# A piece of the first K load goes ahead of wq in a cached GQA decode kernel

## The chip, the cores and the metric

One core of one Trainium2 chip (trn2), in a decode kernel with grouped-query attention (GQA): 16 query heads share 8 heads of K and V. The metric is the device time of one launch in microseconds (us), median over runs. All runs quoted here are of the fast state; a ratio is the mean time of one kernel's fast runs over that of the other's of the same rounds, so it is not quite the ratio of the medians that stand beside it.

## The reference, cut to what matters

```python
# A: x (1,1,448), wq (448, 4096), 16 query heads, 8 KV heads, cache 65536 long, head width 256, all bf16
q = x @ wq
scores = einsum(q, k_cache) * 256 ** -0.5     # k_cache, v_cache: (1, 8, 65536, 256), 268 MB each
a = einsum(softmax(scores), v_cache) @ wo     # wo (4096, 448)
b = token_mlp(layernorm(x))                   # small
out = g * a + (1 - g) * b                     # g = sigmoid(sum(x * gate_w))
```

One token reads two caches of 268 MB. Everything else is small.

## The kernel before

The cache is handled in 32 blocks of 16,384 positions (128 tokens for each of 128 partitions). SP, the engine that issues nearly all DMAs, alternates K and V loads of 8.39 MB. PE, the matmul engine, transposes K in 8 chunks of 16 tokens, forms the scores, and at the end of the block multiplies with V. A K load waits until the first four chunks of the block before are transposed, a V load until the products with the V block before are done. The first block is special: its K comes in two halves, and its V buffer holds wq until the q-projection is over.

```python
@block.sync
def _(eng):
    eng.dma_start(wq_a..., A_wq[0:384]...).then_inc(sem_wq, 16)      # 3072 KB
    eng.dma_start(wq_b,    A_wq[384:448]...).then_inc(sem_wq, 16)    # 512 KB
    for j in range(NP):                                              # 32 blocks
        last = j == NP - 1
        if j >= 1:
            eng.wait_ge(sem_tr[NB - 1], BODY * (j - 1) + DC)         # BODY 8, DC 4
        if j == 0:
            load(kring, A_k_cache, j, HV, NV, 0, sem_k)              # first half of K, 64 tokens
            load(kring, A_k_cache, j, 0, HV, 0, sem_kb)              # second half
        ...                                                          # (cut: last block)
        else:
            load(kring, A_k_cache, j, 0, NV, HV * (j % 2), sem_k)
        if j == 0:
            eng.wait_ge(s_q, 1); eng.wait_ge(s_hb, 1)                # q done: wq's place is free
        else:
            eng.wait_ge(sem_pv, j)
        load(vbuf, A_v_cache, j, ...)
        ...                                                          # (cut: wo, output)

@block.tensor
def _(pe):
    ...                                      # (cut) columns of x
    pe.wait_ge(sem_wq, 32)
    ...                                      # q-projection: 128 matmuls, then s_q
    ...                                      # h row, s_h; clears
    with nc.Fori(...):                       # blocks
        def transposes(k, c, j, u16, x2):    # chunk k of a block
            if k == 0:
                pe.wait_ge(sem_k, u16)       # 16 at block 0
            if k == DC:
                pe.wait_ge(sem_kb, 16)
            ...
```

The softmax here doesn't subtract the row's maximum and nothing guards it: scores larger than these inputs give would overflow.

## Time and profile before

| | before |
|---|---|
| median of 3 runs | 1266.03 us (1266.0 to 1266.64) |
| span of the profiled run | 1264.0 us |
| bytes moved, mean rate | 544.39 MB, 431 GB/s |
| PE, PEld (PE's weight loads), ACT (scalar engine), DVE (vector engine) busy | 73%, 69%, 43%, 33% |
| mean granted clock of PE | 0.842 |

Read it from the bottom: no compute engine is busy all the time, while the DMA row shows nine tenths in every slice but the last. The prediction shows the lines.

### The profile page before, as it was taken

The numbers are of one execution on the slowest core, as the hardware profiler recorded it, in microseconds if no ns is written. First come the engines' busy times: TensorE is split into PE (matmuls) and PEld (weight loads), VectorE is DVE, ScalarE is ACT, GpSimd is POOL, SyncE is SP. The second block draws the span as 40 slices with busy tenths as digits, with TensorE's granted clock in tenths as the row PEclk, the third lists the DMA queues.
The fourth block names the chain that finished last, engine by engine and source line by source line (L and its number), as shares of the span: only waits on it lengthen the run. The fifth ranks groups of instructions, "written<-read, shape, count | busy, mean of one in ns | idle before, by whom it ended". The sixth has DMA issues, their size and how long they took to land.

```text
span 1264.0 us, 38850 instructions
## 1 busy us (share of the span) xinstructions
PE 917.0 (73%) x17114; PEld 868.4 (69%) x17114; DVE 422.5 (33%) x764; ACT 538.2 (43%) x788; POOL 0.9 (0%) x7
## 2 busy tenths in 40 slices
PE   3876678766778667786676876758767688676688
PEld 2766668766677666786666876658766578666687
DVE  2433344333444333443222332323322233332233
ACT  1443345533355433454333553335533355433455
POOL 0000000000000000000000000000000000000000
PEclk9887788787898887987888987889887888877999
DMA  9999999999999999999999999999999999999998
GB/s 411 428 434 436 433 431 431 431 438 431 433 433 433 433 431 438 425 433 440 431 436 429 431 431 433 440 433 433 431 431 431 438 436 433 431 433 431 431 427 367
DMA packets 11623, 544.39 MB, mean 431 GB/s; under 512 B 1369, under 2 KB 1628, under 8 KB 2908
## 3 DMA queue, kind: packets, MB, share of 16 engines
q1 hardware_dynamic: 11522, 544.22, 99.7%
q8 instruction: 8, 0.13, 0.0%
q10 hardware_dynamic: 90, 0.01, 0.0%
q14 instruction: 3, 0.02, 0.0%
HBM read 544.22 MB, written 0.00 MB: 431 GB/s over the span
## 4 chain that ended last, share of the span: by engine, by line
DMA 70%; PE 29%; issue 1%; SPq 0%; DVEq 0%; DVE 0%; ACT 0%; ACTq 0%
DMA kring<-in_A_k_cache_dram 68%; PE kst L298 24%; PE sps L318 4%; DMA wo_sb<-in_A_wo_dram 2%; PE acc L358 0%; SPq L231 0%; SPq L265 0%; SPq L228 0%; SPq L226 0%; PE prj L405 0%; PE acc L347 0%; DVEq L92 0%; DVE out_row L634 0%; ACT pT L658 0%; ACTq L658 0%
## 5 line engine op out<-in xcount | busy, mean ns | idle before, releaser
L298 PE MATMUL kst<-ident,kring 128*128 128x128 f32 x4096 | 563.7, 299 | 304.9 <-DMA kring<-in_A_k_cache_dram 294.1
L669 ACT ACTIVATE ktT<-kst 128x1024 bf16<-128x1024 bf16 x512 | 500.0, 1021 | 667.3 <-PE kst L298 666.5
L298 PEld LDWEIGHTS kst<-ident,kring 128*128 128x128 f32 x4096 | 514.0, 156 | 314.8 <-issue 312.2
L569 DVE COPY ktT<-kst 128x1024 bf16<-128x1024 bf16 x512 | 354.2, 692 | 765.0 <-PE kst L298 742.0
L318 PEld LDWEIGHTS sps<-qcur,ktT 128*128 128x128 bf16 x8192 | 237.8, 96 | 4.1 <-issue 1.6
L318 PE MATMUL sps<-qcur,ktT 128*128 128x2 bf16 x8192 | 236.6, 163 | 1.3 <-issue 1.3
L358 PE MATMUL acc<-vbuf,pT 128*2 128x256 bf16 x4080 | 140.4, 305 | 3.8 <-issue 3.3
L358 PEld LDWEIGHTS acc<-vbuf,pT 128*2 128x2 bf16 x4080 | 105.2, 93 | 30.6 <-issue 3.8
L658 ACT ACTIVATE pT<-sps 128x32 f32 x256 | 51.8, 202 | 16.4 <-PE sps L318 16.4
L347 PE MATMUL acc<-pT,ones_sq 128*128 128x32 bf16 x256 | 11.7, 178 | 12.3 <-ACT pT L658 12.3
L347 PEld LDWEIGHTS acc<-pT,ones_sq 128*128 128x128 bf16 x256 | 8.6, 96 | 15.2 <-ACT pT L658 14.9
L675 ACT ACTIVATE z_b<-z_b 128x448 bf16<-128x448 bf16 x14 | 8.1, 577 | 20.5 <-DVE z_b L556 20.4
L575 DVE COPY accs<-acc 128x288 f32<-128x288 f32 x8 | 3.7, 458 | 38.5 <-PE acc L358 38.5
L394 PEld LDWEIGHTS acc<-sel,accs 128*64 128x64 f32 x112 | 10.8, 214 | 0.9
L394 PE MATMUL acc<-sel,accs 128*64 128x1 f32 x112 | 11.4, 260 | 0.0
L431 PE MATMUL acc<-vbuf 42*128 42x42 bf16 x1 | 0.2, 214 | 8.3 <-DMA b_b<-in_B_b_dram 8.3
L405 PE MATMUL prj<-wo_sb,oTn 128*1 128x112 bf16 x128 | 3.7, 244 | 3.1 <-DVE oTn L600 2.9
L431 PEld LDWEIGHTS acc<-vbuf 42*128 42x128 bf16 x1 | 0.1, 102 | 8.4 <-DMA b_b<-in_B_b_dram 8.4
L562 DVE TENSOR_TENSOR gu<-wtmp,z_b 128x448 bf16<-128x448 bf16 x14 | 5.5, 393 | 1.0
L554 DVE TENSOR_TENSOR z_b<-u_b,wtmp 128x448 bf16<-128x448 bf16 x14 | 5.5, 393 | 1.0
L550 DVE TENSOR_TENSOR z_b<-wtmp,u_b 128x448 bf16<-128x448 bf16 x14 | 5.5, 393 | 1.0
L548 DVE TENSOR_TENSOR wtmp<-u_b 128x448 bf16<-128x448 bf16 x14 | 5.5, 392 | 1.1
(89 smaller groups left out, 82.5 us busy)
## 6 DMA issues: line engine op xcount, KB each, us to landing
kring<-in_A_k_cache_dram SPq DMA_DIRECT2D x4, 4096.0 KB, 24.3
vbuf<-in_A_v_cache_dram SPq DMA_DIRECT2D x1, 6144.0 KB, 25.7
wo_sb<-in_A_wo_dram SPq DMA_DIRECT2D x7, 448.0 KB, 27.6
vbuf<-in_A_wq_dram SPq DMA_DIRECT2D x1, 3072.0 KB, 10.2
vbuf<-in_A_v_cache_dram SPq DMA_DIRECT2D x1, 1024.0 KB, 27.8
vbuf<-in_A_v_cache_dram SPq DMA_DIRECT2D x1, 768.0 KB, 28.9
vbuf<-in_A_wq_dram SPq DMA_DIRECT2D x1, 512.0 KB, 10.9
vbuf<-in_A_v_cache_dram SPq DMA_DIRECT2D x31, 29.7
```

Source lines behind the costliest of these rows:

```text
L298: ins = pe.transpose(kst[:, b, i * P:(i + 1) * P], kring_f[:, at + NT * (k % DC) + 4 * b + i, :], ident[:, :])
L318: ins = pe.matmul(sps[:, par, 2 * nt:2 * nt + 2], ktT[:, par, b, ntl * DH + dj:(ntl + 1) * DH:2], qcur[:, dj, :], start=(dj == 0), stop=(d ...
L347: pe.matmul(acc[:, DENC:SELC], ones_sq[:, :], pT[:, r, :], start=False, stop=(r == BODY - 1), skip_group_check=True)
L358: ins = pe.matmul(acc[o:o + REP, 0:DH], pT[:, r, 2 * nt:2 * nt + 2], vbuf[:, n, :], start=False, stop=False, skip_group_check=True)
L394: ins = pe.matmul(dst[hh * HP:(hh + 1) * HP, i:i + 1], accs[:, i:DH:2 * REP], sel[:, hh:hh + 1], start=False, stop=True, skip_group_check= ...
L548: vec.tensor_tensor(W, U, U, op=ALU.mult)
L550: vec.tensor_tensor(Z, W, U, op=ALU.mult)
L554: vec.tensor_tensor(Z, U, W, op=ALU.add)
L569: vec.tensor_copy(ktT[:, k % KTB, b, :], kst_b[:, b, :]).then_inc(sem_ev[b], 1)
L658: act.activation(pT[:, bass.ds(p0 + k % DC, 1), :].rearrange("p o n -> p (o n)"), sps[:, k % 2, 0:2 * NT], AF.Exp, scale=scale).then_inc(s ...
L669: act.activation(ktT[:, k % KTB, b, :], kst_b[:, b, :], AF.Copy).then_inc(sem_ev[b], 1)
L675: act.activation(z_b[:, :], z_b[:, :], AF.Tanh).then_inc(s_tanh, 1)
```

## The change

The intent: let the first bytes of K arrive first, so that the long work on K is not behind the 3.67 MB of wq. The first half of K is cut in two loads; the first of them, 32 of 64 tokens per partition (2.10 MB), is issued ahead of wq, the rest behind it. PE gets a wait for the new semaphore ahead of its loop.

```diff
+    NLEAD = 32
+        sem_lead = new_sem("sem_lead")
         def _(eng):
-            eng.dma_start(wq_a..., A_wq[0:WF * P, :]...).then_inc(sem_wq, 16)
-            eng.dma_start(wq_b, A_wq[WF * P:DM, :]...).then_inc(sem_wq, 16)
 ...
                 if j == 0:
-                    load(kring, A_k_cache, j, HV, NV, 0, sem_k)
+                    load(kring, A_k_cache, j, HV, HV + NLEAD, 0, sem_lead)
+                    eng.dma_start(wq_a..., A_wq[0:WF * P, :]...).then_inc(sem_wq, 16)
+                    eng.dma_start(wq_b, A_wq[WF * P:DM, :]...).then_inc(sem_wq, 16)
+                    load(kring, A_k_cache, j, HV + NLEAD, NV, 0, sem_k)
                     load(kring, A_k_cache, j, 0, HV, 0, sem_kb)
 ...
+            pe.wait_ge(sem_lead, 16)
             x2_reg = pe.alloc_register("x2_reg")
```

More of the change, by code (lines that the diff above doesn't have):

```diff
@@ L225, in _ @@
         def _(eng):
-            eng.dma_start(wq_a.rearrange("p j n -> p (j n)"),
-                          A_wq[0:WF * P, :].rearrange("(p j) n -> p (j n)", p=P)).then_inc(sem_wq, 16)
-            eng.dma_start(wq_b, A_wq[WF * P:DM, :].rearrange("r (a n) -> (r a) n", a=2)
-                          ).then_inc(sem_wq, 16)
             def load(dst, cache, j, n0, n1, at, sem):
@@ L238, in _ @@
                 if j == 0:
-                    load(kring, A_k_cache, j, HV, NV, 0, sem_k)
+                    load(kring, A_k_cache, j, HV, HV + NLEAD, 0, sem_lead)
+                    eng.dma_start(wq_a.rearrange("p j n -> p (j n)"),
+                                  A_wq[0:WF * P, :].rearrange("(p j) n -> p (j n)", p=P)).then_inc(sem_wq, 16)
+                    eng.dma_start(wq_b, A_wq[WF * P:DM, :].rearrange("r (a n) -> (r a) n", a=2)
+                                  ).then_inc(sem_wq, 16)
+                    load(kring, A_k_cache, j, HV + NLEAD, NV, 0, sem_k)
                     load(kring, A_k_cache, j, 0, HV, 0, sem_kb)
```

## The prediction

> **What bounds the kernel now.** I read the page from the top: engines, slices, queues. The reader is to see that no compute engine is near full and that the DMA row is.
>
> ```profile
> PE 917.0 (73%) x17114; PEld 868.4 (69%) x17114; DVE 422.5 (33%) x764; ACT 538.2 (43%) x788; POOL 0.9 (0%) x7
> ...
> DMA  9999999999999999999999999999999999999998
> ...
> DMA packets 11623, 544.39 MB, mean 431 GB/s; under 512 B 1369, under 2 KB 1628, under 8 KB 2908
> ...
> q1 hardware_dynamic: 11522, 544.22, 99.7%
> ```
>
> K and V cache alone are 2 x 8 x 65536 x 256 x 2 bytes = 537 MB of these 544 MB. 544.39 MB at 431 GB/s is 1263 us, the whole span (1264.0). So the time is bytes over rate, plus the little that the ends cost. The chain of waits agrees if it is read with care: it gives 68% to K loads and 24% to the transposes of L298, but these alternate only because a K load is issued when the transposes have freed its buffer.
>
> ```profile
> 1.67 21.40 DMA kring<-in_A_k_cache_dram
> 23.06 4.34 issue
> 27.41 6.17 PE kst L298 x32
> ...
> 38.79 34.06 DMA kring<-in_A_k_cache_dram
> 72.85 0.13 issue
> 72.97 5.59 PE kst L298 x32
> ...
> 83.77 27.79 DMA kring<-in_A_k_cache_dram
> ```
>
> A full K load is 8.39 MB, 19.5 us at 431 GB/s. The one issued at 83.77 takes 27.79 us, so it stood in the queue for about 8 us before its bytes moved. That is the reserve: PE could release a buffer 8 us later (less the start-up of a transfer) and no DMA engine would pause. I therefore do not read the 24% as PE time to be won.
>
> Where is DMA not full? The table of stretches (us, PE, PEld, DVE, ACT and POOL busy, clock, DMA share, GB/s) answers:
>
> ```profile
> 0.00:4.00 4.00, 0.43 (x5) 0.29 (x5) 2.08 (x11) 0.69 (x1) 0.91 (x7) 1.00 0.65 197
> 4.00:12.00 8.00, 0.21 (x1) 0.10 (x1) 2.56 (x8) 0.60 (x1) 0.00 (x0) 1.00 1.01 427
> 12.00:24.00 12.00, 4.69 (x132) 3.87 (x132) 2.65 (x15) 1.69 (x3) 0.00 (x0) 1.00 1.01 436
> 24.00:53.50 29.50, 24.36 (x404) 23.74 (x408) 13.88 (x26) 17.13 (x25) 0.00 (x0) 0.99 1.03 439
> 53.50:73.00 19.50, 6.95 (x129) 3.95 (x121) 0.53 (x2) 0.00 (x0) 0.00 (x0) 0.59 0.99 426
> ```
>
> Only the first 4 us fall short (197 against some 433, so about 2.2 us lost), and the last 6 us after the final V bytes. In 4 to 73 us, the whole stretch that the change can touch, DMA is at 426 to 439 although PE idles. A change of order there can't win time; it can only lose it by opening a gap.
>
> **What the Trainium skill says.** "DMA: Bandwidth & Descriptors", section "Where 436 GB/s comes from", gives 435 GB/s as the fabric ceiling; the trace agrees, 431 over the span, so there is no headroom of rate. The same page, "Queues, rings and completion order", says each DMA engine takes descriptors in ring order and that the completion count lands when the slowest engine has. The trace agrees: wq (3072 KB, issued 0.74) lands after 10.2 us, the first K half (4096 KB, issued 1.67) after 21.4, the second K half after 30.6: in the order of issue. So moving an issue moves landings and not the sum. "Runtime: NRT & Kernel Launch", section "Terms", says that an engine's instruction memory is refilled in 16 KiB blocks; the trace has 8 packets of 0.13 MB on the instruction queue, 16 KB each. I use this below for the 4.34 us of "issue".
>
> **The change part by part.**
>
> 1. The issue order. Before: wq (3.15 MB), rest of wq (0.52), K first half (4.19), K second half (4.19). After: K lead (32 of its 64 tokens per partition, 128 x 32 x 512 bytes = 2.10 MB), wq, rest of wq, K rest (2.10), K second half. The sum to the end of K's first half is 7.86 MB in both, so the K rest lands where the K half landed, at 23.1 us, and everything behind it is unmoved too.
>
> 2. What it adds: one DMA issue on SP, 0.41 us by those at 0.74 and 1.20, beside a queue that is filled for tens of us; 128 more row packets (two of 16 KB where one of 32 KB was) and 16 completion writes, 144 on 11623. If the 1369 packets under 512 B cost anything visible the rate could not be 431 throughout; I put under 0.1 us.
>
> 3. What the lead buys: nothing that I can find. PE's new wait for it stands after the q-projection and ahead of the loop, and the loop's first block still waits for the count of the old K semaphore (16 at block 0), which now the K rest raises. The transposes can't begin on the lead alone. The new wait is met long before: by the GB/s of the stretches (0.79 MB by 4 us, then 0.427 MB per us) the lead's 2.10 MB are in at 4 + 1.31/0.427 = 7.1 us, and PE gets there past 20.
>
> 4. What it costs: wq comes 2.10 MB later, 2.10/0.43 = 4.9 us. Its last part landed at 1.20 + 10.9 = 12.1, so now at about 17.0. The q-projection began at 12.58, held by the copy of xcol and not by wq; now wq holds it, so the delay is 17.0 - 12.6 = 4.4 us. The 128 matmuls of L441 and L443 end at 16.16 before, 20.6 after; the V load, issued at 17.54 behind the q and h steps, goes out at about 22.0.
>
> Is that delay on the path? First test: V must be in the queue before the K second half ends, at 32.8. Reserve before 15 us, after 11. Second: PE enters the loop at 22.3 instead of 17.9. Before, it could have begun at 23.06 but did so at 27.41; I take the 4.34 us for the first fetch of the loop's instructions (the queue shows instruction packets in 18 to 19, 24 to 25 and 30 to 31 us). If that fetch starts when PE arrives, the transposes start 4.4 us later, at 31.8, and the next K load goes out at 43.2 instead of 38.79. V and the wo load keep the queue filled until 53.5 (wo issued 17.91, 35.6 to landing). Reserve 10 us, before 15. Third: the next V load goes out when PE is done with block 0, at 63.58; 4.4 later is 68.0, and K block 1 lands at 72.85. Reserve 4.9 us, before 9.3. After that PE has to wait for K at 72.85 as before (it idled 6.85 us there, now some 2.5), and from 72.97 on the two kernels are the same. The delay is eaten by idle time of PE.
>
> Sum: 0 from bytes, +0.1 for packets, 0 from the delay: 1266.0 + 0.1 = 1266.1 us.
>
> **Rivals.**
> A. The lead starts PE early and the first block ends sooner. For it: transposes are the longest item of PE (563.7 us), and PE idles 9.5 us ahead of the first. Against: the old wait is kept, and even a PE 5 us earlier would only issue K block 1 sooner into a queue with 15 us of work. Worth 0; time 1266.
> B. The delay starves the queue. The third reserve is the thin one, 4.9 us less the 2 us or so that a transfer needs to its first bytes (the first packets of the kernel end near 2 us, issued at 0.74). If PE's later start grows by more instruction stalls (there are others of 3.33 and 2.38 us in block 0), a gap of 1 to 4 us opens once: 1267 to 1270, 0.1% to 0.3%.
> C. The start-up loss of 2.2 us changes, because the first packets are now 16 KB of K and not 24 KB of wq. It could move either way by under 1 us: 1265 to 1267.
> D. PE meets the loop straight out of the q-projection, so the granted clock of the first blocks differs. It is 1.00 there before; off the path by the same reserves. 0.
>
> **Range and chances.** The three runs before span 0.64 us. A and D give nothing, B is at most +4 at perhaps one in ten, C is within 1. I say 1266.1, eight in ten between 1265.2 and 1267.6. Two per cent is 25 us, ten times the largest loss I can construct and more than the whole time outside DMA's full rate (2.2 + 6 us): 0.5% faster, 99% same, 0.5% slower.
>
> **What would show it.** In the profile after: q-projection first at 16.5 to 17.5 us, its idle time now put to wq; V issued at 21.5 to 22.5; K rest landed near 23; transposes from 27.4 (fetch not tied to PE's arrival) to 32; K block 1 issued by 44 and landing at 72.9 within 0.5; GB/s between 4 and 73 us still about 430; idle before the second block's transposes shorter by what the first lost. Wrong if a slice below 400 GB/s appears between 20 and 75 us, if K block 1 lands 1 us or more later than 72.85, or if transposes start before the K rest has landed.

## The result, and the profile after

After: 1265.9 us median of 6 runs (1265.54 to 1267.22); before, the same rounds: 1266.1 of 6 (1265.96 to 1266.64). Ratio 0.9999, 95% interval 0.9986 to 1.0012: the same time.

The page of the kernel after (engines, bytes, the main queue):

```profile
PE 919.5 (73%) x17112; PEld 865.6 (68%) x17114; DVE 422.5 (33%) x764; ACT 537.0 (42%) x788; POOL 0.9 (0%) x7
...
DMA packets 11767, 544.39 MB, mean 430 GB/s; under 512 B 1385, under 2 KB 1644, under 8 KB 2924
...
q1 hardware_dynamic: 11666, 544.22, 99.6%
```

The same bytes at the same rate, in 144 packets more, as counted: 128 rows and 16 completions.

The chain of waits of the kernel after in its first 90 us (start, duration, what):

```profile
1.67 15.04 DMA vbuf<-in_A_wq_dram
...
22.10 10.15 issue
32.25 6.31 PE kst L302 x32
...
43.77 28.76 DMA kring<-in_A_k_cache_dram
72.53 0.13 issue
72.66 6.58 PE kst L302 x32
```

Set it beside the chain of before. The chain now begins with wq, because the q-projection really waits for it. PE comes to its loop at 22.10 (before about 17.9), the first transposes start at 32.25 (before 27.41), and the next K load is issued at 43.77 (before 38.79). Yet that load lands at 72.53, where it landed at 72.85 before. Five microseconds went into the start of PE's work and none came out at the other end: the 28.76 us of that load against 34.06 before are only less time in the queue. (The run after that was profiled is the slowest of its six; more on that below.)

The table of stretches of the kernel after (us, PE, PEld, DVE, ACT, POOL busy, clock, DMA share, GB/s):

```profile
4.00:12.00 8.00, 0.00 (x0) 0.00 (x0) 1.69 (x6) 0.65 (x1) 0.00 (x0) 1.00 1.03 438
12.00:24.00 12.00, 4.89 (x133) 3.97 (x133) 3.52 (x16) 1.69 (x3) 0.00 (x0) 1.00 1.01 430
24.00:53.50 29.50, 21.25 (x316) 21.12 (x316) 10.18 (x15) 14.29 (x21) 0.00 (x0) 1.00 1.03 439
53.50:73.00 19.50, 10.64 (x213) 7.02 (x212) 4.21 (x13) 2.83 (x5) 0.00 (x0) 0.71 0.99 415
```

PE's work moved from the third stretch to the fourth (316 and 213 matmuls against 404 and 129), into time in which it idled before. GB/s is level except in the last stretch, 415 against 426. That dip is small, and it is in a run that took 1267.22, the slowest of the six. The V load of block 1 shows where it comes from. First before, then after, from the timeline of SP (start, duration, engine and line, operation):

```profile
63.58 0.33 SPq L231 DMA_DIRECT2D vbuf<-in_A_v_cache_dram  x1
```

```profile
68.59 0.33 SPq L230 DMA_DIRECT2D vbuf<-in_A_v_cache_dram  x1
```

The trace records 16 landings for a large load; I read them as one for each of the 16 DMA engines (the landings named here are read one by one from the packed traces). K block 1, which stands ahead of that V load, ended on its first engine at 70.76 and on its last at 72.85 before; after, at 70.67 and 72.53. So V was issued 7.2 us ahead of the first engine running dry before, and 2.1 us after. I call this lead of an issue over the end of the work ahead of it the reserve. From this V load on the last engine lands 1.4 us later than in the run before (93.58 against 92.20), the mean of the sixteen 0.4 us later (91.58 against 91.18). The spread between first and last engine grew from 1.9 us to 3.0 and stayed so to the end. That is a small loss, once, in this run. It is also where the run's time is settled: over the profiled runs of before, of the change and of ten experiments below (all but e7 and e8), whose times go from 1265.56 to 1280.62, the time less the last landing of this V load is always 1173.5 to 1174.1 us. To within that half microsecond, what makes these kernels differ has happened by then.

### The profile page after: what moved, and what is told of

The parts are those of the page before. It is cut to its first block, busy times and chain, and to the rows that moved or that the text cites. A ratio compares the mean times of both kernels' runs of the same rounds, so it can differ in the third digit from the quotient of the medians.

```text
span 1265.3 us, 38849 instructions
## 1 busy us (share of the span) xinstructions
PE 919.5 (73%) x17112; PEld 865.6 (68%) x17114; DVE 422.5 (33%) x764; ACT 537.0 (42%) x788; POOL 0.9 (0%) x7
## 4 chain that ended last, share of the span: by engine, by line
DMA 70%; PE 28%; issue 1%; SPq 0%; DVE 0%; DVEq 0%; ACT 0%; ACTq 0%
DMA kring<-in_A_k_cache_dram 66%; PE kst L302 23%; PE sps L322 4%; DMA wo_sb<-in_A_wo_dram 2%; DMA vbuf<-in_A_wq_dram 1%; PE acc L362 0%; PE sps L445 0%; SPq L230 0%; PE sps L447 0%; DVE hbT L614 0%; PE prj L451 0%; SPq L269 0%; SPq L239 0%; PE acc L351 0%; PE prj L403 0%
## 5 line engine op out<-in xcount | busy, mean ns | idle before, releaser
L302 PE MATMUL kst<-ident,kring 128*128 128x128 f32 x4096 | 554.9, 296 | 299.2 <-DMA kring<-in_A_k_cache_dram 287.8
L302 PEld LDWEIGHTS kst<-ident,kring 128*128 128x128 f32 x4096 | 505.0, 154 | 309.3 <-issue 306.4
L362 PE MATMUL acc<-vbuf,pT 128*2 128x256 bf16 x4080 | 152.1, 321 | 3.2 <-issue 2.8
L362 PEld LDWEIGHTS acc<-vbuf,pT 128*2 128x2 bf16 x4080 | 111.4, 98 | 35.5 <-issue 3.3
L398 PE MATMUL acc<-sel,accs 128*64 128x1 f32 x112 | 11.4, 260 | 0.0
L445 PE MATMUL sps<-xcol,vbuf 128*128 128x1 bf16 x96 | 3.5, 165 | 4.0 <-DMA vbuf<-in_A_wq_dram 4.0
L445 PEld LDWEIGHTS sps<-xcol,vbuf 128*128 128x128 bf16 x96 | 3.5, 104 | 4.1 <-issue 4.1
L565 DVE TENSOR_SCALAR z_b<-z_b 128x448 bf16<-128x448 bf16 x14 | 3.9, 277 | 5.9 <-ACT z_b L680 5.9
```

The costliest lines, as they stand in the source:

```text
L302: ins = pe.transpose(kst[:, b, i * P:(i + 1) * P], kring_f[:, at + NT * (k % DC) + 4 * b + i, :], ident[:, :])
L362: ins = pe.matmul(acc[o:o + REP, 0:DH], pT[:, r, 2 * nt:2 * nt + 2], vbuf[:, n, :], start=False, stop=False, skip_group_check=True)
L398: ins = pe.matmul(dst[hh * HP:(hh + 1) * HP, i:i + 1], accs[:, i:DH:2 * REP], sel[:, hh:hh + 1], start=False, stop=True, skip_group_check= ...
L445: pe.matmul(sps[:, 1, j:j + 1], wq_a[:, kt, col + dj:col + DH:2], xcol[:, kt:kt + 1], start=(kt == 0), stop=False)
L565: vec.tensor_scalar(Z, Z, 1.0, None, op0=ALU.add)
```

## The experiments

All twelve kernels gave the reference's result. The theory: the time is bytes over rate as long as the DMA queue never runs dry; the change delays PE by some 4 to 5 us, which idle time of PE absorbs, and the thinnest reserve is ahead of the second V load. The rivals: a gain is hidden by the kept wait, a cost of the split hides a gain, or the start never matters at all. Each set has its own runs of before: 1266.19 in the first (e1 to e4) and 1266.2 in the second (e5 to e8), on one chip, and 1265.86 in the third (e9 to e12), on another.

**e1_split_only.** The split and the new wait without the new order.

```diff
+            eng.dma_start(wq_a...)      # wq back at the head of the queue
+            eng.dma_start(wq_b...)
             load(kring, A_k_cache, j, HV, HV + NLEAD, 0, sem_lead)
-            eng.dma_start(wq_a...); eng.dma_start(wq_b...)
             load(kring, A_k_cache, j, HV + NLEAD, NV, 0, sem_k)
```

> wq first as before, the first K half in two loads of 32 tokens, PE waits for both. Theory (bytes over rate, reserves): 1266.0 to 1266.3, under 0.1 us for 144 packets and one issue; PE reaches the loop at 17.9 and starts the transposes at 27.4 as before. Rival (two smaller loads cost rate): more than 1266.7, and GB/s of 4 to 24 us below 425.

1266.25 (1266.06 to 1266.56, 5 runs) against 1266.19 (9 runs), ratio 1.0000 (0.9987 to 1.0014). Transposes at 27.41. The split costs nothing that can be seen, so it hides no gain that could be seen either.

**e2_lead_used.** The first block begins on the lead alone.

```diff
                 if k == 0:
-                    pe.wait_ge(sem_k, u16)
+                    pe.wait_ge(sem_lead, 16)
+                    with pe.If(j > 0):
+                        pe.wait_ge(sem_k, u16)
+                if k == NLEAD // NT:
+                    pe.wait_ge(sem_k, u16)
```

> The change, with the first block waiting for the lead alone and for the K rest only at its third chunk. Theory: PE reaches the loop at about 22.1, with the K rest landed (21.6), and begins transposes near 32.2 as in the change: 1265.5 to 1266.5. Rival (the kept wait hid a gain): transposes begin before 27 us and the time falls by the 4 to 5 us that block 0 then wins, 1261 to 1262.

1265.84 (1265.56 to 1266.24, 5 runs), ratio 0.9997 (0.9983 to 1.0011). Transposes begin at 31.47. With the kept wait gone the lead is still of no use: when PE gets to its loop (22.09), the K rest has landed too (21.59), and the next 9.38 us go to something else than this data (see e12). This does not show what PE could do with a lead if it were free at 8 us; what a PE earlier by 5 us is worth is shown by before against after: nothing that can be seen.

**e3_wq_after_half and e4_wq_last.** More of the same delay, as edits of the kernel before: wq behind the whole first half, then behind both.

```diff
-            wq_a, wq_b ahead of the loop
                     load(kring, A_k_cache, j, HV, NV, 0, sem_k)
+                    wq_a, wq_b                                    # e3
                     load(kring, A_k_cache, j, 0, HV, 0, sem_kb)
+                    wq_a, wq_b                                    # e4, instead
```

> wq behind the whole first K half: twice the delay of the change. Theory (a reserve of 3.9 us is left in the change ahead of the second V load, and a transfer needs some 2 us to start): q-projection from 21.5, V issued at 26.5, transposes from 37, second V load issued at 73.5 against K block 1 landed at 72.5, a gap of 2 to 3 us: 1268 to 1269.5. Rival (the start never matters, bytes over rate only): 1266. Second rival (transposes start when data land, not when instructions come): transposes by 31, no gap, 1266.

> wq behind both halves of the first K block. Theory: q-projection from 31.5, V issued at 36.5, queue empty from 32: a gap of 5 to 7 us there, a small one ahead of K block 1 (issued near 58.5) and 4 to 6 us ahead of the second V load (issued near 83): 1276 to 1282; transposes from 47. Rival (bytes over rate only): 1266. Second rival (only the V gap counts): 1271 to 1273.

e3: 1268.65 (1267.85 to 1270.82, 5 runs), ratio 1.0023 (1.0009 to 1.0037). e4: 1275.85 (1274.03 to 1277.51, 4 runs), ratio 1.0071 (1.0056 to 1.0087), just under the range that I gave. So the start does matter once the reserve is used up, and "bytes over rate only" is out. In e3 the second V load was issued at 70.87, after the first engine had ended K block 1 (70.58). In e4 the stretches show the two holes (same columns as above):

```profile
32.00:37.00 5.00, 3.94 (x110) 3.11 (x107) 1.05 (x4) 0.00 (x0) 0.00 (x0) 1.00 0.01 3
37.00:57.00 20.00, 11.49 (x150) 11.47 (x151) 5.54 (x8) 7.25 (x10) 0.00 (x0) 1.00 1.01 422
77.00:82.00 5.00, 4.45 (x87) 2.57 (x79) 0.00 (x0) 0.00 (x0) 0.00 (x0) 0.61 0.31 125
```

3 GB/s while the q-projection ends and V can't be issued (issued at 36.20, wq landed at 31.14), 125 GB/s ahead of the second V load (issued at 81.27, K block 1 landed at 80.89). The first transposes stand at 35.94 in e3 and 45.51 in e4, although K's first half had landed at 13.14 and 13.03 us. The start of the transposes follows PE's arrival at the loop (26.93, 36.53) by 9.0 us and does not follow the data.

**e5_lead16, e6_lead48, e9_lead8.** The size of the lead.

```diff
-    NLEAD = 32
+    NLEAD = 16        # e5;  48 in e6;  8 in e9
```

> The change with a lead of 16 tokens: wq is late by 2.45 us and not 4.9. Theory: inside the reserve, V issued near 19.4, transposes near 29.5, 1265.5 to 1266.5. It also looks at the 0.3 us by which the two kernels with the lead first stood below before (1265.84 and 1265.9 against 1266.2): if the smaller first packets cause it, it should be here too, 1265.6 to 1265.9; if it is chance, 1266.0 to 1266.4.

> The change with a lead of 48 tokens: wq late by 7.3 us. Theory: second V load issued near 71, 1.5 us before K block 1 lands, which is less than a transfer's start-up of about 2 us: 1266.0 to 1267.5, between the change (1265.9) and the lead of 64 (1268.65).

> The change with a lead of 8 tokens (0.52 MB, 4 KB packets first), wq late by 1.2 us. A lead of 16 gave 1265.63 in runs that did not overlap those of before (1265.22 to 1265.86 against 1266.02 to 1266.45), a mere split with wq first 1266.25. If smaller packets at the very start are what is gained: 1265.3 to 1265.8. If it came from where the instruction fetches fall among the 16 engines: anything from 1265.5 to 1266.4, with the spread of an engine's landings between 1.7 and 2.3 us.

e5: 1265.63 (1265.22 to 1265.86, 6 runs) against 1266.2 (10 runs), ratio 0.9995 (0.9983 to 1.0008). e6: 1267.47 (1265.76 to 1268.57, 5 runs), ratio 1.0007 (0.9993 to 1.0020). e9: 1266.39 (1266.04 to 1266.49, 5 runs) against 1265.86 (9 runs), ratio 1.0003 (0.9989 to 1.0017). e6 lies between the change and e3, as it should. A lead of 16 looked like a gain of half a microsecond, and I tried 8 to see whether the smaller first packets made it: 8 came out half a microsecond slower. That falls as an explanation. All of these intervals hold 1, and what makes 16 and 32 stand 0.2 to 0.6 us below and 8 above I have not found; in the profiled runs the last engine lags the first by 2.1 us (before), 1.9 (16), 1.7 (e2) and 2.2 (8), but one profile each proves nothing.

**e10_after_again.** No edit.

> The change once more, unedited. Its profiled run was its slowest (1267.22), with the second V load issued 2.1 us before the first engine ended K block 1 and the last engine 1.4 us later from there on; the others had 1265.5 to 1266.2. Theory (the reserve is just touched): most runs 1265.5 to 1266.2, some at 1266.8 to 1267.5; median 1265.8 to 1266.3. Rival (that run was a disturbance): all within 1265.5 to 1266.2.

1265.62 median; four runs at 1265.37 to 1265.67 and the profiled one at 1268.04. Ratio 0.9997 (0.9983 to 1.0011). The median is a hair under what I gave and the high run above it; the two groups are there. In the profiled run the second V load was issued at 69.91. Put together from the profiled runs:

| kernel | V of block 1 issued | K block 1 ends, first engine | reserve | mean landing of V block 1 | time of that run |
|---|---|---|---|---|---|
| before | 63.58 | 70.76 | 7.2 us | 91.18 | 1266.10 |
| e2 | 65.15 | 70.82 | 5.7 | 91.12 | 1265.86 |
| after | 68.59 | 70.67 | 2.1 | 91.58 | 1267.22 |
| e10 | 69.91 | 70.65 | 0.7 | 92.57 | 1268.04 |
| e6 | 70.18 | 70.71 | 0.5 | 92.59 | 1268.57 |
| e3 | 70.87 | 70.58 | -0.3 | 92.46 | 1267.85 |

With 5.7 us or more nothing is lost, with 2.1 us or less 1 to 2.5 us; no row lies between (e7 and e11 fill that gap). The change sits on the edge. Both of its profiled runs fell over it and none of its nine others did. Whether profiling itself adds the stalls of PE that decide it, I can't tell from so few; the profiled e2 has the same order of loads and did not fall over, and in e6 a run that was not profiled took 1268.12. What moves the second V issue within one order of loads is PE's way through block 0: from the issue of K block 1 to that of V block 1 it took 22.3 us in e2, 24.8 in the change (as in before) and 26.1 in e10.

**e7_k_late2, e8_k_late4, e11_k_late1.** The reserve of a block in the middle of the run, measured on the kernel before by issuing every K load later.

```diff
-    eng.wait_ge(sem_tr[NB - 1], BODY * (j - 1) + DC)
+    eng.wait_ge(sem_tr[NB - 1], BODY * (j - 1) + DC + 2)    # e7;  + 4 in e8;  + 1 in e11
```

> Before, but every K load from block 1 on is issued two chunks of transposes later, 2 x 2.59 = 5.2 us. Theory (8 us of queue stand ahead of a K load in every block): 16.1 us after a block's transposes begin, V has 3.4 us left to run: no gap, 1265.5 to 1267. Rival (the chain's 24% of transposes is on the path): 30 x 5.2 = 156 us more, 1420.

> As the last, but four chunks later, 10.4 us, more than the reserve. Theory: K issued 21.3 us after the block's transposes begin, V done after 19.5: with some 2 us of start-up a gap of 3 to 4.5 us in each of 30 blocks: 1355 to 1400. Rival (queue order hides any such delay): 1266. The chain's reading: 30 x 10.4, 1578.

> Before, with the K loads issued one chunk (2.6 us) later. Mended theory: the reserve runs to the first of the 16 engines that ends the V load, not to the landing; it is 440.66 - 434.83 = 5.8 us in a block of the profile of before, so 3.2 us are left here and 0.6 in the run with two chunks, which lost 18 us. Needed are some 2 to 3 us: 1265.8 to 1268. Rival (any delay of a K load costs its share): half of the loss of two chunks, 1275.

e7: 1284.46 (4 runs) against 1266.2, ratio 1.0146 (1.0131 to 1.0162): my expectation of no loss failed. e8: 1415.45 (4 runs), ratio 1.1178 (1.1161 to 1.1195), 15 us above the range I gave. e11: 1266.03 (4 runs) against 1265.86, ratio 1.0001 (0.9986 to 1.0017).

The reading of the chain as "transposes are 24% of the path" is refuted by e11: 2.6 us more ahead of 30 K loads, and no loss. My own reserve of 8 us less 2 for start-up was too generous, as e7 shows. The chain around one K load of e7, then of e8:

```profile
444.21 21.88 DMA kring<-in_A_k_cache_dram
466.09 0.12 issue
466.21 3.89 PE kst L298 x17
```

```profile
446.23 21.75 DMA kring<-in_A_k_cache_dram
467.99 0.12 issue
468.11 1.96 PE kst L298 x8
```

A load that finds an empty queue (e8) takes 21.75 us, which is what a load costs with its start-up; that is 2.4 us more than the 19.35 us between the mean landings of loads that follow each other without a gap (before). A load of before took 27.79 us with the time in the queue. In e7 that load was issued at 444.21; the V load ahead of it ended on its last engine at 446.74 and on its first at 445.77. 2.5 us to the landing would have been enough by my reckoning; 1.6 us to the first engine was not: this load landed, in the mean, 0.3 us later than without a gap. Over the run e7 lost (1284.46 - 1266.2) / 30 = 0.6 us a block.

One block is not the run, so here are the 29 full K loads of e7 from block 2 on. Eleven had less than 1.6 us to the first engine, and each lost 0.3 to 2.3 us. Fifteen had 1.8 to 2.7 us: thirteen lost 0.25 us or less, two lost 1.0 and 1.2. Three had over 3.1 us and lost nothing. These losses sum to 16 us of the 18. In e11 the same 29 loads had 2.8 to 5.4 us to the first engine, and none lost more than 0.05. Counted to the last engine the order is worse: among loads of e7 with 2.9 to 3.2 us to the landing are ones that lost nothing, 0.6 and 2.2 us. So the reserve has to be counted to the first engine; here less than 1.6 us was never enough, 1.8 to 2.7 mostly, and 2.8 always.

**e12_wq_last_quiet.** e4 with the V load held back until PE has transposed its first chunk, so that PE enters its loop with no transfer under way.

```diff
                     eng.wait_ge(s_hb, 1)
+                    eng.wait_ge(sem_tr[NB - 1], 1)
```

> wq last, and V of block 0 issued only when PE has transposed the first chunk, so that no other transfer is in the queue while PE fetches the first instructions of the loop. If the 9 to 10 us between PE's arrival and the first transpose are instruction packets that stand behind K and V packets: below 4 us here, transposes from 38 to 41. Rival (a fixed cost of the loop's entry): 9 us again, transposes from 45. Time 1274 to 1282 in the first case, 1282 to 1290 in the second.

1280.89 (4 runs), ratio 1.0118 (1.0103 to 1.0134). The stretch (columns as above) and the chain:

```profile
32.00:38.00 6.00, 3.92 (x109) 3.09 (x106) 1.05 (x4) 0.00 (x0) 0.00 (x0) 1.00 0.02 5
```

```profile
36.51 3.85 issue
40.36 6.07 PE kst L299 x32
```

With the queue empty the "issue" ahead of the first transposes is 3.85 us, against 8.97 in e4 at the same place with V in the queue. The instruction packets fit: they start at 34.03, 37.47 and 40.73 here, 3.3 to 3.4 us apart; at 23.36, 29.45 and 35.45 in the run after, some 6 us apart; and in all of before, after, e4 and e12 the transposes start 1.7 to 1.8 us after the second of them has ended (24.58 + 1.07 and 27.41; 29.45 + 1.10 and 32.25; 42.84 + 0.97 and 45.51; 37.47 + 1.20 and 40.36). The other kernels do the same (1.7 us), except e2, which has an added branch there (2.0). So the wait that the profile calls "issue" is, by all that these runs show, PE waiting for its instructions, and most of it is made by the data traffic: e12 differs from e4 only in the held V load. The packets themselves take 1.0 to 1.2 us either way; it is their start that comes late. That they stand in the queue behind data packets is the likely reading; no view shows the queue itself.

## Why the prediction was right, point by point

**Time.** 1266.1 said, 1265.9 measured, and the mechanism is the one given: DMA bound, the same bytes at the same rate, a delay taken up by PE's idle time. e3 and e4 show that this was a matter of reserves and not of a law. That the number came so close has some luck in it: the reserve was on the edge, and nine of eleven runs of the change stayed on the good side.

**The delay.** Said: q-projection from 17.0, V issued at 22.0, loop at 22.3, transposes at 31.8, K block 1 issued at 43.2, second V at 68.0. Measured: 16.84, 21.78, 22.10, 32.25, 43.77, 68.59. That the 4.34 us of "issue" were a fetch that begins with PE's arrival was a guess from instruction packets. e3 and e4 confirm that the transposes follow PE's arrival and not the data, and e12 that the wait hangs on the traffic. That the fetch begins with the arrival they don't confirm: the first packet starts 0.8 us after it in before and 1.3 after it in the change, but 2.0 and 2.5 us ahead of it in e4 and e12. Not foreseen: the copy of xcol came later too (13.88 against 12.37), because the small loads it hangs on landed later (12.54 against 11.03). wq was later still, so it cost nothing. Smaller misses: the lead landed at 8.30 and not at 7.1; the K rest landed at 21.60 and not at 23.1, since the 23.06 of before was one late engine, the other fifteen having ended by 21.83; PE's idle time at block 1 was 1.56 us and not 2.5.

**The kept wait.** Right that the lead buys nothing. But the wait was the lesser reason: e2 took it away and nothing changed, because PE reaches its loop after the K rest has landed.

**Packets.** "+0.1 us" is below what can be measured; e1 has it at 0.06 between medians.

**The third reserve: mis-sized.** Said 4.9 us less about 2. (The packets that end near 2 us, from which the 2 was taken, are those of small loads; the first rows of wq end at 3.37. The 2.4 us of e8 is the better figure.) Measured in the run after: 3.9 us to the landing of K block 1, but 2.1 us to its first engine, and this is the number that counts. The prediction took the landing, which is the last of sixteen engines, as the end of the queue. The same slip is in the opening remark that PE could release a buffer 8 us later less the start-up: e7 did so by 5.2 us and lost 18 us. The term to put in its place is the time to the first engine, 5.3 to 7.6 us in the blocks of before, of which between 2 and 3 us are needed. Rival B was there: two of eleven runs of the change show it, 1.0 and 2.4 us over the slowest of their others, inside its 1 to 4. Eleven runs are too few to say whether one in ten was wrong. In e10 it came as B had it, PE's delay growing on the way: the transposes started 4.7 us later than in before, the second V load 6.3.

**Rival C** (the start-up moves the time by under 1 us) is not shown in the times; e5 and e9 point in opposite directions. The landings hint at it: the first wo load, which has the same bytes ahead of it whatever their order, landed in the mean at 52.11 to 52.25 in five profiles with wq first, at 51.90 to 52.09 in six with at least 16 tokens of K first, and at 52.38 with a lead of 8. That is 0.2 us or so either way, as the medians of e2, e5 and e9 go, from one profile each.

No version beats both kernels clearly. e5 has the lowest median beside its own before (ratio 0.9995), inside the noise.

## What to carry to other kernels

When a kernel is bound by bytes, as here, reordering its first loads redistributes waiting: ask of each issue that moves how long before the queue runs dry it still comes, and look for a loss before a gain. Count that reserve to the first DMA engine that runs out of work, not to the landing, which is the last; in this kernel 3 us were enough. And give the first pass through a loop its own look: its instructions come by DMA too, and with data in the queue PE waited 8.8 to 11.4 us for its first matmul there, without it 3.85 us.

## What the Trainium skill lacked or had wrong

- "DMA: Bandwidth & Descriptors", section "Where 436 GB/s comes from": it says that for HBM to SBUF the HBM side, about 358 GB/s, binds. With one core running, this kernel holds 431 GB/s over 1264 us, near the fabric figure of 435 that the same section gives. The skill does not lack this: the same page, section "Measured (HBM→SBUF, 128 partitions, SWDGE, issued from GpSimd)", gives about 358 GB/s for each of two cores that stream together. The sentence quoted here wants "with both cores".
- The same page, "Why a DMA increments its semaphore by 16 and not by 1", says that the engines finish independently. It does not say what follows for a queue that must not run dry: first and last engine were 2.1 us apart from the first V load to the end of the run before, and K loads issued less than 1.6 us before the first engine ended lost 0.3 to 2.3 us each (e7), those issued 2.8 us or more before it nothing (e11).
- "Runtime: NRT & Kernel Launch", section "Terms", has the 16 KiB refill blocks right (8 packets, 0.13 MB). The same page, section "Instruction fetch mechanics", calls the cost of crossing a block "mostly hidden" and names stalls at taken branches, without a time. Here it was not hidden on the first pass of the loop, and no page that I found has a time for it beside data traffic: the first two blocks came 5.6 to 8.3 us apart with the queue full and 3.4 us apart with it empty, and PE waited 8.8 to 11.4 us against 3.85 us between its arrival at its loop and the first matmul there.
